# Attention backward: one dS unit in eight transposed by TensorE, with three smaller moves of loads and stores

## The chip, the cores and the metric

One core of one Trainium2 chip. The metric is the device time of one execution in microseconds. The kernel before took 2856.8 us (median of three runs, 2853.1 to 2865.4).

Names of engines in the profile: PE is TensorE's matmuls, PEld its weight loads, DVE is VectorE, ACT is ScalarE, POOL is GpSimd, SPq is the queue of DMA commands that SyncE issues. L1286 is a line of the kernel that ran; the changed kernel has other line numbers than the kernel before, so each fence says whose lines it shows. "..." in a fence or in code marks what is left out. The "built program" is the list of instructions that a kernel is built into.

## The reference, cut to what matters

A transformer block with adaptive layer norm (S = 2048, D = 512, 32 heads of 16, F = 1792, bf16), forward and all gradients.

```python
def _A_ref(x, wqkv, wo):                      # attention
    ...
    scores = einsum('bhqd,bhkd->bhqk', q, k) * scale
    p = softmax(scores)
    return einsum('bhqk,bhkd->bhqd', p, v)... @ wo
def _B_ref(x, w1, b1, w2, b2):                # MLP with squared relu
    ...
x = x + ga * _A_ref(layernorm(x) * (1 + ca) + sa, wqkv, wo)
x = x + gb * _B_ref(layernorm(x) * (1 + cb) + sb, w1, b1, w2, b2)
# returned: x and the gradients to x, wqkv, wo, w1, b1, w2, b2, c, w_mod
```

The argument is about the backward of the attention. For each head, each chunk of 512 keys and each block of 128 queries it recomputes the scores and their exp, forms dP = dO V^T, then dS = P * dP, and uses dS twice: as it is for dK, and transposed for dQ. The transposed dS is the tile `dsT`.

## The kernel before

A "unit" is two heads by 128 queries by 512 keys; there are 1024 of them in the backward. Four units make a group (G = 4), and one DMA transpose turns the whole group. `stp` gives two score buffers of one PSUM bank each, `dpp` two dP buffers of two banks each; with one bank each for `acckv` and `accq` all eight banks are used.

```python
dtp = tile_pool(name="p5dt", bufs=4)                       # dsT
stp = tile_pool(name="p5st", bufs=2, space=PSUM)           # scores
dpp = tile_pool(name="p5dp", bufs=2, space=PSUM)           # dP
...
def turn(g, jp, kvT):                       # 16 times in all: dK, dV of two heads
    tp = dpp.tile([P, ST, P], BF16, name="dp")
    for st in range(ST):
        nc.tensor.transpose(tp[:, st, :], kvT[:, st * P:(st + 1) * P], self.ident[:])
    ...                                     # two copies out by ACT
def dS(dp, u):
    (T, g, jp, c, ib, kvT, pu, dsg, i) = u
    nc.vector.tensor_tensor(dsg[:, i], dp[:], pu[:], ALU.mult)
    pend.append((T, g, jp, c, ib, kvT, pu, dsg[:, i]))
    if i == G - 1:
        dsT = dtp.tile([P, 8 * G, P], BF16, name="dsT")
        nc.sync.dma_start_transpose(dsT[:], dsg[:].rearrange("p i a k -> p (i a k)"))
        for i in range(G):
            pendq.append((T, g, jp, c, ib - G + 1 + i, i, dsT))
...
for i in range(G):                          # the loop over the units of a group
    for a in range(2):
        stt = stp.tile([P, 512], F32, name="st")
        nc.tensor.matmul(stt[:], lhsT=T["QT"][rs, q], rhs=masked["KT"]...)     # scores
        if last:
            dP(dp, last, a)                                                    # dP of the unit before
        nc.scalar.activation(pu[:, a, :], stt[:], ACT.Exp, scale=self.scale)
    if last:
        dS(dp, last)
    last = (T, g, jp, c, ib, kvT, pu, dsg, i)
    if i % 2 == 1 and len(pend) >= 4:
        r = kv_two()                        # dV and dK of two units
        ...
    elif i % 2 == 0 and len(pendq) > 2 * G:
        for _ in range(4 if len(pendq) > 3 * G else 2):
            dq(pendq.pop(0), [0, 1])        # 8 matmuls each, on dsT
```

The softmax here doesn't subtract the row's maximum and nothing guards it: scores larger than these inputs give would overflow.

## Time and profile before

| | before |
|---|---|
| time, median | 2856.8 us |
| backward, first to last score matmul | 1454.8 us |
| waits for dsT (as the view of that tile adds them) | 337.7 us, 238 times |
| TensorE at half clock from the first score to the last dq, in whole windows of 3.41 us | 170.7 us |
| from the last score matmul to the end | 145.9 us |

The prediction shows the lines that this rests on. One more view is used, the busy time in one stretch inside the backward. Its columns are the stretch, its length, busy microseconds (and instructions) of each engine, TensorE's mean granted clock, the busy share of the DMA engines and what they moved in GB/s. For the kernel before:

```profile
core 0: us, PE busy (x) PEld busy (x) DVE busy (x) ACT busy (x) POOL busy (x), PEclk, DMA share, GB/s
1300.00:2700.00 1400.00, 1227.44 (x15997) 502.25 (x15997) 1209.69 (x1062) 1079.93 (x1999) 0.00 (x0) 0.94 1.14 203
```

To see: the clock of 0.94, and 203 GB/s with the DMA engines' share above one (transfers overlap).

### The profile page before, as it was taken

To read this page: it belongs to the slowest core of one execution; us is meant where nothing else is said; L and a number is where in the kernel's file an instruction comes from. 1 tells how busy PE (TensorE), PEld (TensorE's weight loads), DVE (VectorE), ACT (ScalarE), POOL (GpSimd) and SP (SyncE) were. 2 spreads that over 40 slices of the span, in tenths; PEclk is the share of its full clock that TensorE was granted. 3 is DMA by queue.
4 is the path that set the end of the run, shared out by engine and by line. 5 is a ranking of instruction groups with operands and counts; after the bars stand their busy time and mean duration, and the time that the engine had idled before them with its cause. 6 is when DMAs were issued, how large, how long until landed. Compare 5 with 4: busy or idle time off the path is not lost. (4 is left out here: it accounts for less than half of the span.)

```text
span 2853.7 us, 72244 instructions
## 1 busy us (share of the span) xinstructions
PE 2530.8 (89%) x29963; PEld 1218.3 (43%) x30186; DVE 1787.2 (63%) x2712; ACT 2214.1 (78%) x3376; POOL 360.7 (13%) x633
## 2 busy tenths in 40 slices
PE   5999799999999989978888898888988889889887
PEld 2555455555555545723333333333333333333343
DVE  4222423323322335648898888888988889889747
ACT  4999899999999974248787777787877778778623
POOL 2244202211311223420000000000000000000021
PEclk9999899999999999989899999999999999999999
DMA  4367733511531357989999999999999999999977
GB/s 149 88 147 161 172 70 107 123 45 40 137 83 43 100 151 175 194 192 201 211 195 203 203 196 209 199 201 210 196 208 203 199 209 198 204 204 205 214 194 187
DMA packets 1331345, 472.86 MB, mean 166 GB/s; under 512 B 1266470, under 2 KB 1293608, under 8 KB 1331016
## 3 DMA queue, kind: packets, MB, share of 16 engines
q1 hardware_dynamic: 1299816, 379.40, 72.5%
q0 software_dynamic: 29088, 86.21, 10.4%
q8 instruction: 236, 3.87, 0.5%
q10 hardware_dynamic: 2112, 2.62, 0.3%
q14 instruction: 93, 0.76, 0.1%
HBM read 83.30 MB, written 67.11 MB: 53 GB/s over the span
## 5 line engine op out<-in xcount | busy, mean ns | idle before, releaser
L1269 ACT ACTIVATE pu<-st 128x512 bf16<-128x512 f32 x2048 | 1108.3, 595 | 313.8 <-PE dp L1218 279.6
L1223 DVE TENSOR_TENSOR ds<-dp,pu 128x1024 bf16<-128x1024 f32 x1024 | 1213.1, 1220 | 198.2 <-PE dp L1218 161.9
L331 ACT ACTIVATE pu<-st 128x1024 bf16<-128x1024 f32 x1024 | 955.7, 1046 | 22.5 <-PE st L328 18.0
L328 PE MATMUL st<-QTm,KTq 128*128 128x512 bf16 x1940 | 586.5, 379 | 37.2 <-ACT pu L331 7.5
L293 PEld LDWEIGHTS <-pu 128*128 128x128 bf16 x8192 | 344.9, 96 | 245.8 <-issue 20.5
L1265 PE MATMUL st<-m,q 64*128 64x512 bf16 x1024 | 371.4, 404 | 21.4 <-ACT pu L1269 9.6
L1265 PE MATMUL st<-m,QTq 64*128 64x512 bf16 x1024 | 365.0, 396 | 16.0 <-ACT pu L1269 4.4
L1218 PE MATMUL dp<-m,q 64*128 64x512 bf16 x1024 | 373.5, 408 | 0.0
L1199 PEld LDWEIGHTS <-dsT 128*128 128x128 bf16 x8192 | 241.1, 97 | 307.1 <-DMA dsT<-ds 189.8
L1218 PE MATMUL dp<-m,dOTq 64*128 64x512 bf16 x1024 | 366.4, 401 | 0.0
L293 PE MATMUL accbank<-Vaug,pu 128*128 128x17 bf16 x8192 | 349.3, 171 | 18.3 <-DVE O L301 11.4
L328 PEld LDWEIGHTS <-KTq 128*128 128x128 bf16 x2048 | 194.9, 96 | 205.8 <-issue 140.7
L1199 PE MATMUL accq<-Kg,dsT 128*128 128x16 bf16 x4096 | 143.6, 171 | 83.1 <-DMA dsT<-ds 82.8
L1199 PE MATMUL accq<-q,dsT 128*128 128x16 bf16 x4096 | 144.5, 171 | 65.6 <-DMA dsT<-ds 65.1
L1434 POOL DMA_DIRECT2D wmod<-in_w_mod_dram x6 | 4.6, 772 | 1462.1 <-DVE kvT L1182 1455.9
L1179 PE MATMUL acckv<-ds,q 128*16 128x512 bf16 x1024 | 165.3, 405 | 0.0
L1179 PE MATMUL acckv<-pu,q 128*16 128x512 bf16 x1024 | 165.3, 405 | 0.0
L1179 PE MATMUL acckv<-ds,Qg 128*16 128x512 bf16 x1024 | 162.1, 398 | 0.7 <-DVE ds L1223 0.7
L1179 PE MATMUL acckv<-pu,dOg 128*16 128x512 bf16 x1024 | 162.1, 398 | 0.0
L1218 PEld LDWEIGHTS <-q 64*128 64x128 bf16 x1024 | 90.8, 94 | 112.0 <-issue 101.4
L1218 PEld LDWEIGHTS <-dOTq 64*128 64x128 bf16 x1024 | 89.8, 94 | 103.3 <-issue 94.1
L300 DVE RECIPROCAL rl<-accbank 128x4 f32<-128x4 f32 x128 | 23.0, 179 | 164.8 <-PE accbank L293 164.7
(309 smaller groups left out, 2345.3 us busy)
## 6 DMA issues: line engine op xcount, KB each, us to landing
KTq<-KTq_d POOLq DMA_DIRECT2D x24, 512.0 KB, 3.6
duT_d<-auT POOLq DMA_DIRECT2D x4, 1792.0 KB, 8.3
aT_d<-rT POOLq DMA_DIRECT2D x4, 1792.0 KB, 13.0
KTq_d<-KTq SPq DMA_DIRECT2D x32, 128.0 KB, 2.1
QTq_d<-ev_fm SPq DMA_DIRECT2D x32, 128.0 KB, 2.4
VTq_d<-vT POOLq DMA_DIRECT2D x4, 1024.0 KB, 6.6
O_d<-O POOLq DMA_DIRECT2D x4, 1024.0 KB, 5.4
m<-KTq_d SPq DMA_DIRECT2D x32, 128.0 KB, 3.7
```

The costliest lines, as they stand in the source:

```text
L293: nc.tensor.matmul(acc[:, a, sub, :], lhsT=pu[:, a, sub * P:(sub + 1) * P], rhs=Vaug[:, kb, h, :], start=(kb == 0 and a == 0 and sub == 0) ...
L300: nc.vector.reciprocal(self.rl[:, st0:st0 + 4, h], acc[:, a, :, DH])
L328: nc.tensor.matmul(stt[:, a, :], lhsT=KT[:, kb * P:(kb + 1) * P], rhs=QTm[2 * jp + a][:], start=True, stop=True)
L331: nc.scalar.activation(pu[:], stt[:], ACT.Exp, scale=self.scale)
L1179: nc.tensor.matmul(acckv[r:r + DH, :], lhsT=T[n][:, ib, col:col + DH], rhs=src[:, a, :], start=(ib == 0), stop=(ib == ST - 1))
L1199: nc.tensor.matmul(accq[:, ib, a, :], lhsT=dsT[:, (i * 2 + a) * 4 + sub, :], rhs=T["K"][:, 4 * c + sub, col:col + DH], start=(c == 0 and i ...
L1218: nc.tensor.matmul(dp[:, a, :], lhsT=T["dOT"][rd, ib * P:(ib + 1) * P], rhs=masked["VT"][2 * jp + a][rd, 512 * c:512 * (c + 1)], start=Tru ...
L1223: nc.vector.tensor_tensor(dsg[:, i], dp[:], pu[:], ALU.mult)
L1265: nc.tensor.matmul(stt[:], lhsT=T["QT"][rs, q], rhs=masked["KT"][2 * jp + a][rs, c0:c0 + 512], start=True, stop=True)
L1269: nc.scalar.activation(pu[:, a, :], stt[:], ACT.Exp, scale=self.scale)
L1434: nc.gpsimd.dma_start(wmod[:], wmod_v[:, :, j * D:(j + 1) * D])
```

## The change

The intent: take load off the queue of DMA transposes, which bounds the backward, by letting TensorE turn one unit in eight (the first unit of every second group). Three small parts come with it: the load and scaling of W2 in three parts in the forward, all four weight tiles for dx loaded at once in the transition, and in the tail an earlier start of the dx tiles and a store on another queue.

```diff
             def dS(dp, u):
-                    dsT = dtp.tile([P, 8 * G, P], BF16, name="dsT")
-                    nc.sync.dma_start_transpose(dsT[:], dsg[:].rearrange("p i a k -> p (i a k)"))
+                    i0 = len(grp)
+                    dsT = grp[0] if i0 else dtp.tile([P, 8 * G, P], BF16, name="dsT")
+                    nc.sync.dma_start_transpose(dsT[:, 8 * i0:, :], dsg[:, i0:].rearrange("p i a k -> p (i a k)"))
 ...
+            def turn_ds(dsg, grp):
+                dsT = dtp.tile([P, 8 * G, P], BF16, name="dsT")
+                tp = stp.tile([P, 8, P], BF16, name="st")
+                for b in range(8):
+                    nc.tensor.transpose(tp[:, b, :], dsg[:, 0, b // 4, b % 4 * P:(b % 4 + 1) * P], self.ident[:])
+                nc.scalar.copy(dsT[:, 0:4, :], tp[:, 0:4, :])
+                nc.vector.tensor_copy(dsT[:, 4:8, :], tp[:, 4:8, :])
+                grp.append(dsT)
 ...
+                                if i == G - 1 and ib0 // G % 2:
+                                    turn_ds(dsg, grp)
 ... W2, in gen_weights and gen_weights_2
-        nc.sync.dma_start(w2[:], io["B_w2"].rearrange("(ft p) j -> p ft j", p=P))
+        self.load_w2(0, 5)
 ...
-        for ft in range(FT):
-            nc.vector.tensor_tensor(w2[:, ft, :], w2[:, ft, :], self.mod_row(5), ALU.mult)
-            if ft % 2:
-                yield 0
+        cuts = [0, 5, 10, FT]
+        for (a, b) in zip(cuts, cuts[1:]):
+            if b < FT:
+                self.load_w2(b, min(b + 5, FT))
+            for ft in range(a, b):
+                nc.vector.tensor_tensor(w2[:, ft, :], w2[:, ft, :], self.mod_row(5), ALU.mult)
+            yield ("wait", 4)
 ... dx weights: w_kt from a pool of four buffers, all loads and scalings first, transposes later
 ... tail
-            for _ in range(8):
+            for _ in range(5):
                 run("b", gb)
 ...
-            nc.sync.dma_start(io["out_9"]..., o[:])
+            nc.gpsimd.dma_start(io["out_9"]..., o[:])
```

More of the change, by code (lines that the diff above doesn't have):

```diff
@@ L720, in last_chunk @@
         fill.until("half")
-        self.load_bwd()
-        for _ in self.load_wmt():
-            fill.take(13)
+        ws = self.load_wmt(self.open_pool("wkt", bufs=1))
+        self.T0, pieces = self.load_group(0)
+        pieces = self.pair_pieces(0, 0) + pieces
+        for n, (d, sr) in enumerate(pieces):
+            nc.sync.dma_start(d, sr)
+            fill.take(7)
+            if n % 3 == 2 and ws:
+                self.turn_wmt(*ws.pop(0))
+        for w in ws:
+            self.turn_wmt(*w)
         fill.drain()
-        for name in ("dw2", "dw1", "e0", "dwps", "tps", "mps"):
+        for name in ("wkt", "dw2", "dw1", "e0", "dwps", "tps", "mps"):
             self.close_pool(name)
@@ L857, in gen_weights, with load_w2 @@
             yield 0
+    def load_w2(self, a, b):
+        self.nc.sync.dma_start(self.w2[:, a:b, :], self.io["B_w2"].rearrange("(ft p) j -> p ft j", p=P)[:, a:b, :])
     def gen_weights_1(self):
@@ L1100, in open_bwd, with load_wmt @@
         self.qp = self.open_pool("p5q", bufs=1, side="right")
-    def load_bwd(self):
-        nc = self.nc
-        self.T0, pieces = self.load_group(0)
-        for (d, sr) in self.pair_pieces(0, 0) + pieces:
-            nc.sync.dma_start(d, sr)
-    def load_wmt(self):
+    def load_wmt(self, sb):
         nc, io = self.nc, self.io
@@ L1112, in load_wmt, with turn_wmt @@
         self.WmT = self.wp.tile([P, 3 * DT, D], BF16, name="WmT")
+        ws = []
         for kt in range(DT):
-            w = self.wp.tile([P, 3 * D], BF16, name="w_kt")
+            w = sb.tile([P, 3 * D], BF16, name="w_kt", bufs=DT)
             nc.sync.dma_start(w[:], io["A_wqkv"][kt * P:(kt + 1) * P, :])
             nc.scalar.activation(w[:], w[:], ACT.Copy, scale=self.opcaT[:, kt:kt + 1])
-            yield
-            nc.sync.dma_start_transpose(self.WmT[:, :, kt * P:(kt + 1) * P], w[:])
-            yield
+            ws.append((kt, w))
+        return ws
+    def turn_wmt(self, kt, w):
+        self.nc.sync.dma_start_transpose(self.WmT[:, :, kt * P:(kt + 1) * P], w[:])
     def load_group(self, g):
@@ L1215, in dP @@
             def dP(dp, u, a):
-                (T, g, jp, c, ib, kvT, pu, dsg, i) = u
+                (T, g, jp, c, ib, kvT, pu, dsg, i, grp) = u
                 rd = slice(64 - 64 * jp, 128 - 64 * jp)
@@ L1221, in dS @@
             def dS(dp, u):
-                (T, g, jp, c, ib, kvT, pu, dsg, i) = u
+                (T, g, jp, c, ib, kvT, pu, dsg, i, grp) = u
                 nc.vector.tensor_tensor(dsg[:, i], dp[:], pu[:], ALU.mult)
@@ L1251, in attn_bwd @@
                                 nc.sync.dma_start(*pieces.pop(0))
-                            dsg = self.dsp.tile([P, G, 2, 512], BF16, name="ds")
+                            dsg, grp = self.dsp.tile([P, G, 2, 512], BF16, name="ds"), []
                             for i in range(G):
@@ L1271, in attn_bwd @@
                                     dS(dp, last)
-                                last = (T, g, jp, c, ib, kvT, pu, dsg, i)
+                                last = (T, g, jp, c, ib, kvT, pu, dsg, i, grp)
                                 if i % 2 == 1 and len(pend) >= 4:
@@ L1456, in gen_p7 @@
                     nc.scalar.activation(o[:, kt, :], dm[:], ACT.Copy, scale=self.scT[:, kt:kt + 1])
-            nc.sync.dma_start(io["out_9"].rearrange("(kt p) n -> p kt n", p=P)[:, :, j * D:(j + 1) * D], o[:])
+            nc.gpsimd.dma_start(io["out_9"].rearrange("(kt p) n -> p kt n", p=P)[:, :, j * D:(j + 1) * D], o[:])
             for kt in range(DT):
```

## The prediction

> **What bounds the kernel now.** I read the slices of the page first. They split the 2853.7 us into a forward part (to about 1050, ACT full), a transition (to 1258), the attention backward (1258 to 2711) and a tail. The backward is half the time and everything in it looks busy, so I asked for the groups of instructions, then for all that touches the tile dsT, then for the queue of SP and the order of time.
>
> The page and the groups with their shapes kept apart:
>
> ```profile
> PEclk9999899999999999989899999999999999999999
> DMA  4367733511531357989999999999999999999977
> ...
> L1223 DVE TENSOR_TENSOR ds<-dp,pu 128x1024 bf16<-128x1024 f32 x1024 | 1213.1, 1220 | 198.2 <-PE dp L1218 161.9 <-ACT pu L1269 15.6 <-ACT dv_t L1192 1.9
> ...
> L1199 PEld LDWEIGHTS <-dsT 128*128 128x128 bf16 x8192 | 241.1, 97 | 307.1 <-DMA dsT<-ds 189.8 <-issue 117.2
> ```
>
> To see: DMA is at nine tenths or more through the whole backward, and what TensorE waits for is dsT, the transposed dS.
>
> What touches dsT, then the queue of SP in a stretch of the backward:
>
> ```profile
> L1227 SPq DMA_TRANSPOSE dsT<-ds x256: 4777/5246/6183, 1264.0 to 2711.3; - x128
> ...
>   DMA dsT<-ds: 337.7, 238
> ...
> DMA to landing us min/median/max: 6.6/7.7/11.5
> ```
>
> ```profile
> 1896.89 0.57 SPq L1251 DMA_DIRECT2D m<-KTq_d  x1
> 1897.55 5.31 SPq L1227 DMA_TRANSPOSE dsT<-ds  x1
> 1902.92 0.57 SPq L1251 DMA_DIRECT2D m<-KTq_d  x1
> 1903.58 4.92 SPq L1227 DMA_TRANSPOSE dsT<-ds  x1
> 1908.55 0.57 SPq L1251 DMA_DIRECT2D m<-VTq_d  x1
> ```
>
> To see: the queue has no hole. 256 transposes by 5.25 is 1344 us, 121 loads by 0.57 another 71; together 1415 of 1452 us. The queue of transposes is the bound of the backward, by a little.
>
> How small the margin is shows in the order of time. A pair of units (two heads, two blocks of 128 queries) starts at 1900.31 and the next at 1902.73:
>
> ```profile
> 1900.31 0.39 PE L1265 MATMUL st<-m,QTq 64*128 64x512 bf16 x1
> ...
> 1900.73 2.14 ACT L1269 ACTIVATE pu<-st 128x512 bf16<-128x512 f32 x4 [0.28 <-PE dp L1218]
> ...
> 1901.38 0.37 PE L1265 MATMUL st<-m,QTq 64*128 64x512 bf16 x1
> ...
> 1901.87 0.37 PE L1265 MATMUL st<-m,QTq 64*128 64x512 bf16 x1
> ...
> 1902.73 0.39 PE L1265 MATMUL st<-m,QTq 64*128 64x512 bf16 x1
> ```
>
> To see: scores at 0, two exps to 1.49, the last scores of the pair at 1.56 (they need the buffer that the second exp frees), dP and dV/dK, next pair at 2.42. This TensorE-ACT loop gives 512 x 2.42 = 1239 us without any dsT wait. VectorE does a dS every 1.13 us back to back (smallest spacing in the trace), 2.26 per pair, so it sits just under.
>
> I counted all pairs in the trace. The 1450 us of the backward are: 1241 clean loop; about 118 of TensorE standing for dsT; about 46 of half clock (157 us at half clock; a pair wholly in it takes 3.43, so each us costs 0.29); 32 for the 16 turns of kvT (3.76 + 3.08 against 4.84: 2.0 each); some 13 for the rest. 34 of the 40 half-clock stretches begin within 2.2 us after a hole of over 1.3 us in TensorE, nearly always a dsT wait: the clock is lost to the same waits.
>
> **What the Trainium skill says.** "TensorE: Matmul & The Clock Gate", Part 1 (What's actually happening): the clock is either half or full, decided by activity over windows of 3413 ns. The trace agrees: stretches of 3.4 or 6.8 us at 0.5. The same page, Part 4 (PE-mode transpose): a transpose ends in PSUM and must be copied out, and does not count as TensorE activity the same way. The copies are in the trace; that it costs clock is not: 15 of the 16 kvT turns (16 transposes each, with holes of 0.3 to 0.5 about them) are followed by no half clock. "DMA: Bandwidth & Descriptors", Issuing engines are not separate DMA queues: all queues share 16 engines, so moving the stores of the last output to the GpSimd queue gives only order, no bandwidth. And "PSUM — Partial Sum Buffer", Specifications: a bank is 2 KiB per partition; the turned 8 x 128 bf16 fill one, exactly one of the two score buffers.
>
> **The change part by part.**
>
> Backward. In every second group of four units, the first unit is transposed by TensorE, so 128 DMA transposes shrink from 32 blocks to 24: 128 x 5.25/4 = 168 us off the queue. Per eight units it then needs 5.25 + 3.94 + 0.6 of loads = 9.8 us against a clean loop of 9.7; with the turn the loop is longer than the queue, and dsT arrives (0.6 lag + 7.7) before its use two groups later (about 10). The 118 + 46 us of waits and half clock should go, except perhaps 15.
>
> Added are 128 turns: 8 transposes, an ACT copy and a VectorE copy of 128x512. Their rows before are those of the kvT turn and of the forward's turns:
>
> ```profile
> 1349.60 1.05 PE L1188 MATMUL dp<-ident,kvT 128*128 128x128 bf16 x16 [0.28 <-DVE ds L1223]
> ...
> 1350.69 0.58 ACT L1192 COPY dk_t<-dp 128x512 bf16<-128x512 bf16 x1 [1.10 <-PE dp L1188]
> ```
>
> ```profile
> L577 DVE COPY fT<-tp x4: 405/426/426, 1042.5 to 1060.2; 128x512 bf16<-128x512 bf16 x4
> ```
>
> To see: half of the 16 transposes is some 0.54, the copies 0.58 and 0.43. They follow dV/dK at the end of a pair, so the next pair starts 0.54 late. The copies hold one of the two score buffers: ACT copies until 0.69 after that start; VectorE, which stands at its dS until then, until about 0.69 too. The second scores of the next unit thus come at 0.75 instead of 0.23, their exp ends at 1.77, the last scores of the pair come at 1.84 instead of 1.56: another 0.28. (The same working gives 3.08 for the pair after a kvT turn, as measured.) So 0.82 per turn. In half of the turns VectorE is some 0.4 late from a kvT copy (0.74 against 0.16 of slack per pair): 0.36 more. Mean 1.0, in all 128 us, of which I take 122.
>
> New backward: 1241 + 122 + 32 + 13 + 15 = 1423, that is 27 less.
>
> W2 in three parts (around 300 to 370 us). Before, 12 scalings stand ahead of the copy-out of O, and TensorE stands 5.5 us for it:
>
> ```profile
> PE accbank L293 <- DVE O L301: 8.7, 3, 5.5
> ```
>
> In the changed order on VectorE the first scaling stands between the reciprocal and the copy-out of the block before, and there it must wait for its load: 640 of 1792 KB, estimated landing 5 us after issue (10.6 before), then the small b2 load some 3 us later. The copy-out comes some 7 us late, one block earlier than now. The second and third part are loaded after the transpose of Wo and their nine scalings stand ahead of another copy-out: some 5 us more and 2 of half clock. I expect the wait to move and not to go: +5. By the delay, 16 matmuls more are left over after the forward loop: +2.
>
> dx weights in four buffers (1214 to 1258). TensorE stood 9.2 us for a_blk, ACT for each w_kt in turn, and the first exp of the backward waited 4.2 for the last of them. All four loads now go first; the traffic is the same (3.8 MB and eight transposes), only the chain at the end goes: -5.
>
> Tail. The dx tiles start after five blocks instead of eight, and the stores leave the queue that feeds dqT. TensorE is busy 113 us of the last 130, eight or nine of idle at the end can't go; so -5, and -3 because the last dsT (11.5 us after issue now) has 24 blocks.
>
> Sum: -27 + 7 - 5 - 8 = -33, and 2856.8 - 33 = 2824. I go to 2818, because the turns may cost 0.82 throughout.
>
> **The rivals.** (1) The queue was the whole bound and the turns hide in the loop's slack: then -164 + 15 in the backward and about 2700. Against it: the loop has no slack, the score buffer is its critical resource. (2) VectorE becomes the bound: 8 x 1.13 + 0.43 + 0.46 (kvT, dq) = 9.94 per eight units, under 10.7; if its dS is really 1.19 apart it is 10.4, still under. It would give about 2810 to 2830. (3) The turns trip the half clock: 3.4 x 0.29 = 1 us per turn, +128, about 2940. Against it: the kvT turns. (4) The W2 wait does go: 10 us better, about 2808.
>
> **Range and chances.** The size of a turn moves most: 0.25 us either way is 32 us. W2, transition and tail together are good for 15. I give 2778 to 2850. Faster by over 2% (under 2800) needs turns of about 0.8 and one of the small parts to do well: 0.27. Within 2%: 0.70. Slower: 0.03.
>
> **What would show it.** Right: dsT waits under 30 us where they were 338; mean clock of the backward near 0.99 instead of 0.94; pairs with a turn of about 2.96, and 2.70 after it; the queue of SP with holes; a wait for the copy-out of O one block earlier. Wrong: dsT waits over 100 us, pairs longer than 3.3 around a turn, VectorE without holes, or half clock after turns.

## The result, and the profile after

The changed kernel took 2849.5 us (median of four, 2847.6 to 2852.9), against 2857.4 us for the kernel before in the same rounds: ratio 0.9971, interval [0.9946, 0.9995]. Run a second time on another chip in five rounds it gave 0.9981 [0.996, 1.0002]. So the kernel is 5 to 8 us faster, or in the second measurement not told apart from the kernel before; predicted were 39 (2856.8 to 2818). The interval is a 95% interval.

What the change aimed at did happen. The slices of the page of the changed kernel:

```profile
PEclk9999999999999999989999999999999999999999
DMA  4367632520531266989999999999999999999986
```

The same stretch of its backward as above:

```profile
1300.00:2700.00 1400.00, 1271.06 (x17074) 564.47 (x17074) 1259.76 (x1192) 1162.48 (x2135) 0.00 (x0) 1.00 0.99 181
```

The clock is 1.00 and the DMA moves 181 GB/s instead of 203. The view of the tile dsT of the changed kernel (durations are least, median and greatest, in ns):

```profile
L1238 SPq DMA_TRANSPOSE dsT<-ds x256: 3566/4766/5948, 1263.1 to 2705.2; - x128
...
  ACT dsT L1248: 30.4, 81
  DMA dsT<-ds: 9.9, 11
...
DMA to landing us min/median/max: 5.4/6.8/9.4
```

Waits for dsT fell from 337.7 to 9.9 us and the half clock of the backward from 170.7 to 13.7 us (10.2 of it at the very start of the backward, 3.4 after the last score). But the backward, from first to last score matmul, went only from 1454.8 to 1449.3. The gain was spent in the same place.

Where it went shows in the length of pairs of units, counted from the first score matmul after a dV/dK to the next such. A plain pair has no transpose in it or just before it; a kvT turn is the `turn` of dK and dV shown above. I went through all 508 pairs of each trace:

| pair | before | after | after, all such pairs above 2.42 us each |
|---|---|---|---|
| plain | 478 pairs, 2.42 us but up to 6.6 where it waits | 239 pairs, 2.42 us | 4 us |
| ends in a turn of dS | none | 112 pairs, 2.98 us | 66 us |
| starts after a turn of dS | none | 127 pairs, **3.16 us** | 96 us |
| kvT turn | 15 pairs 3.76, then 15 pairs 3.08 | 15 pairs 3.76, then 15 pairs 3.64 (kvT and dS turn) | 38 us |
| sum of all pairs | 1440.9 us | 1435.7 us | |

The prediction had 2.96 for the pair with a turn and 2.70 for the one after it. The first is right, the second is not. The order of time around one turn of the changed kernel (start, length, engine, line; what ended its idle time in brackets):

```profile
1911.79 0.62 PE L1247 MATMUL st<-ident,ds 128*128 128x128 bf16 x8
...
1912.35 0.39 PE L1286 MATMUL st<-m,QTq 64*128 64x512 bf16 x1
...
1912.45 0.58 ACT L1248 COPY dsT<-st 128x512 bf16<-128x512 bf16 x1 [0.48 <-PE st L1247]
...
1913.07 0.42 DVE L1249 COPY dsT<-st 128x512 bf16<-128x512 bf16 x1 [0.29 <-ACT dsT L1248]
1913.59 0.37 PE L1286 MATMUL st<-m,QTq 64*128 64x512 bf16 x1 [0.85 <-ACT pu L1290]
```

To see: VectorE's copy does not run beside ACT's copy, it waits for it. And the second score matmul of the pair, the last line, comes 1.24 us after the first. Its bracket names an exp, and rightly. I looked up in the built program which PSUM bank each of these uses and what it waits for:

```
PE   first scores    -> bank 1, waits for an exp of the unit before
ACT  copy, blocks 0-3 <- bank 0 (the turned tile), waits for PE
DVE  copy, blocks 4-7 <- bank 0, waits for ACT's copy
ACT  exp of the first scores <- bank 1
PE   second scores   -> bank 1 again, waits for that exp
```

This is so at all 127 turns that have scores after them. There are two score buffers. The turned tile has one of them until both copies are done; the other is taken by the first scores, whose exp stands behind the copy in ACT's queue. Over all turns the medians after the start of the pair are: ACT copy 0.10 to 0.69, VectorE copy 0.72 to 1.15, second scores 1.24 (0.05 after that exp, 0.09 after VectorE's copy). Whichever buffer they take, they cannot come much before 1.2. The prediction had both copies done at 0.69 and the scores at 0.75, in the buffer of the turn.

The W2 wait moved and stayed, as predicted. In the view of waits of the changed kernel from 298 to 400 us (total, times, longest):

```profile
PE accbank L293 <- DVE O L301: 9.3, 3, 4.6
```

### The profile page after: what moved, and what is told of

Same layout as the page of the kernel before. It is cut to its first block, busy times and chain, and to the rows that moved or that the text cites. A ratio compares the mean times of both kernels' runs of the same rounds, so it can differ in the third digit from the quotient of the medians.

```text
span 2845.7 us, 74675 instructions
## 1 busy us (share of the span) xinstructions
PE 2590.2 (91%) x31210; PEld 1280.3 (45%) x31210; DVE 1830.7 (64%) x2840; ACT 2293.5 (81%) x3504; POOL 365.0 (13%) x639
## 5 line engine op out<-in xcount | busy, mean ns | idle before, releaser
L1290 ACT ACTIVATE pu<-st 128x512 bf16<-128x512 f32 x2048 | 1125.6, 596 | 210.0 <-PE dp L1228 115.7
L328 PE MATMUL st<-QTm,KTq 128*128 128x512 bf16 x2048 | 611.6, 380 | 30.5 <-ACT pu L331 7.7
L1286 PE MATMUL st<-m,q 64*128 64x512 bf16 x1024 | 362.7, 382 | 68.2 <-ACT pu L1290 61.1
L1228 PE MATMUL dp<-m,q 64*128 64x512 bf16 x1024 | 364.3, 387 | 0.0
L1189 PE MATMUL acckv<-ds,Qg 128*16 128x512 bf16 x1024 | 154.0, 381 | 0.6 <-DVE ds L1233 0.6
L1189 PE MATMUL acckv<-ds,q 128*16 128x512 bf16 x1024 | 154.5, 382 | 0.0
L1189 PE MATMUL acckv<-pu,q 128*16 128x512 bf16 x1024 | 154.5, 382 | 0.0
L1189 PE MATMUL acckv<-pu,dOg 128*16 128x512 bf16 x1024 | 154.0, 381 | 0.0
```

The source lines that it names most:

```text
L328: nc.tensor.matmul(stt[:, a, :], lhsT=KT[:, kb * P:(kb + 1) * P], rhs=QTm[2 * jp + a][:], start=True, stop=True)
L1189: nc.tensor.matmul(acckv[r:r + DH, :], lhsT=T[n][:, ib, col:col + DH], rhs=src[:, a, :], start=(ib == 0), stop=(ib == ST - 1))
L1228: nc.tensor.matmul(dp[:, a, :], lhsT=T["dOT"][rd, ib * P:(ib + 1) * P], rhs=masked["VT"][2 * jp + a][rd, 512 * c:512 * (c + 1)], start=Tru ...
```

## The experiments

Seventeen kernels ran, the changed one twice. "Backward" is the sum of the 508 pairs; the rightmost column is the median of that pair. All give correct results except the two marked as wrong.

| kernel | ratio to before | backward | waits for dsT | pair after a turn |
|---|---|---|---|---|
| before | 1 | 1440.9 | 337.7 | |
| the changed kernel | 0.9971 | 1435.7 | 9.9 | 3.16 |
| turn in a dP buffer, two banks | 0.9796 | 1383.3 | 41.1 | 2.59 |
| the same, one bank | 0.9815 | 1387.1 | 53.9 | 2.59 |
| two PSUM tiles | 0.9802 | 1379.1 | 37.6 | 2.58 |
| half a unit turned | 0.9833 | 1398.8 | 101.4 | 2.66 |
| no turn, 24 blocks by DMA (wrong) | 0.9593 | 1328.9 | 145.8 | |
| no turn, 16 blocks by DMA (wrong) | 0.9375 | 1266.3 | 1.0 | |
| turns alone | 0.9996 | 1438.3 | 17.0 | 3.16 |
| small parts alone | 1.0016 | 1441.0 | 335.9 | |
| dP buffer, VectorE copy alone | 0.9797 | 1384.8 | 49.1 | 2.58 |
| dP buffer, DMA in two pieces | 0.9784 | 1374.0 | 12.7 | 2.68 |
| before, DMA in two pieces | 1.0168 | 1484.2 | 259.1 | |
| dP buffer, one unit in 16 | 0.9822 | 1389.3 | 172.9 | 2.60 |
| VectorE copy, two pieces, no small parts | 0.9774 | 1377.9 | 17.2 | 2.68 |
| two tiles, two pieces, no small parts | 0.9777 | 1374.8 | 16.9 | 2.68 |
| the changed kernel, tail undone | 0.9986 | 1438.5 | 12.2 | 3.16 |
| the changed kernel again | 0.9981 | 1437.5 | 12.1 | 3.16 |

### The turned tile in a dP buffer, its halves in two banks

My first theory came from the Trainium skill, "PSUM — Partial Sum Buffer", section "PSUM bank collisions raise a hardware error": the compiler back end adds a dependency between any two instructions on different engines that touch the same bank and quadrant of partitions, reads included. The halves of the turned tile lie in one bank.

```diff
-                tp = stp.tile([P, 8, P], BF16, name="st")
+                tp = dpp.tile([P, 16, P], BF16, name="dp")
-                    nc.tensor.transpose(tp[:, b, :], ...)
+                    nc.tensor.transpose(tp[:, b // 4 * 8 + b % 4, :], ...)
-                nc.vector.tensor_copy(dsT[:, 4:8, :], tp[:, 4:8, :])
+                nc.vector.tensor_copy(dsT[:, 4:8, :], tp[:, 8:12, :])
```

> The changed kernel with the turned tile in a dP buffer instead of a score buffer, its two halves in two PSUM banks. Theory 'bank': in the changed kernel the turn costs 1.30 us and not 0.82 because both halves of the turned tile lie in one bank that is also a score buffer, so the VectorE copy waits for the ACT copy (0.3 to 0.4 us) and the second scores of the next unit wait for both. Then here the wait of the VectorE copy for ACT is gone from the tile view of dsT, the pair after a turn falls from 3.16 us to 2.70 to 2.80, the pair with a turn stays at 2.98, and the time is 45 to 58 us under the changed kernel, about 2798. Rival 'engine time': the pair is late because ACT spends 0.58 us and VectorE 0.42 us more in it; then the pair after a turn stays at 3.05 to 3.2 and the time is within 12 us of the changed kernel.

Measured: 2793.8 us, ratio 0.9796 [0.9773, 0.9818], the pair after a turn 2.59 us. The gain is there, but not for the reason given. The order of time around a turn:

```profile
1914.31 0.62 PE L1247 MATMUL dp<-ident,ds 128*128 128x128 bf16 x8
...
1914.87 0.39 PE L1286 MATMUL st<-m,QTq 64*128 64x512 bf16 x1
...
1914.97 0.59 ACT L1248 COPY dsT<-dp 128x512 bf16<-128x512 bf16 x1 [0.27 <-PE dp L1247]
...
1915.30 0.39 PE L1286 MATMUL st<-m,QTq 64*128 64x512 bf16 x1
...
1915.59 0.42 DVE L1249 COPY dsT<-dp 128x512 bf16<-128x512 bf16 x1 [0.34 <-ACT dsT L1248]
```

To see: with the halves in two banks VectorE's copy still waits for ACT's (128 of 128 times, 41.5 us in all). But the second scores start 0.43 after the first, before either copy is done: no score buffer is held, so each of the two scores has its own. So the wait is not about the bank, and it costs nothing by itself (the pair is 2.58 in the run below in which the copies overlap).

### The same with one bank

The edit is the first line of the one above only.

> As the run before it, with the turned tile in a dP buffer, but all eight blocks in one bank. It splits the theory in two. If the price is the hold of the score buffer, this kernel does as well as the one with two banks (pair after a turn 2.70 to 2.80, about 2798), though its VectorE copy still waits about 0.3 us for ACT. If the serial copies cost time by themselves, the pair after a turn is 3.0 to 3.1 and the time about 2830. In both cases the wait of the VectorE copy for the ACT copy must be there; if it is not, it is not a matter of the bank.

Measured: 2799.2 us, 0.9815 [0.9793, 0.9837]; the pair after a turn 2.59, the wait of VectorE's copy for ACT's 40.0 us. Same as with two banks within the intervals. What costs is that the turn takes a score buffer; the run with two tiles, below, adds that it is the time for which it is held. The rival that ACT's and VectorE's own time makes the pair late falls: they do the same copies here.

### Half a unit turned

Four blocks, one ACT copy, still in a score buffer; the DMA takes 28 of 32.

```diff
-                for b in range(8):
+                for b in range(4):
...
-                nc.scalar.copy(dsT[:, 0:4, :], tp[:, 0:4, :])
-                nc.vector.tensor_copy(dsT[:, 4:8, :], tp[:, 4:8, :])
+                nc.scalar.copy(dsT[:, 0:4, :], tp[:])
```

> The changed kernel with only the first four of the eight blocks of the unit turned by TensorE, copied by ACT alone, still in a score buffer; the DMA takes 28 of 32 blocks. There is one copy, so nothing to be put in series. Theory: 0.28 us of transposes in the pair with a turn (2.70), a hold of the score buffer until about 0.7 after the start of the next pair, which makes that pair 2.70; 128 x 0.56 = 72 us for all turns instead of 166, and a DMA queue of 1331 us that stays below the loop. With some 20 us for new waits for dsT: 65 to 90 us under the changed kernel, about 2770. Rival: a turn has a fixed price (a hole in TensorE and a late exp), the pair after it stays above 2.95 and the gain is under 40 us; or the DMA queue bounds again and waits for dsT come back to over 60 us.

Measured: 2804.4 us, 0.9833 [0.9809, 0.9857]. The pair after a turn is 2.66 as expected; the pair with a turn is 2.86 in the median, not 2.70. In the built program the second scores go to the buffer of the turn, wait for the one copy (done at 0.67) and come at 0.72. The time is a miss, by 34 us: the waits for dsT came back, which the rival had in part.

```profile
  DMA dsT<-ds: 101.4, 97
```

### No turn, and 24 blocks by DMA (wrong)

The changed kernel without `turn_ds`; dq of that unit reads another unit's blocks, so the result is wrong.

> Wrong on purpose (dq of one unit in eight is summed from another unit's blocks): the changed kernel with its 24-block DMA transposes but with no turn on TensorE and no copies. It shows the price of the turns in place and the clean loop. If the turns cost 1.30 us each as counted by pairs (128 x 1.30 = 166), the time is 2849 - 166 = 2683, pairs are 2.42 throughout but for the kvT turns, and waits for dsT stay under 30 us (queue 1247 us of about 1286). If the turns hide a wait that comes back without them (VectorE at 1.13 us per dS, or the DMA queue), it is above 2720.

Measured: 2736.0 us, 0.9593 [0.9572, 0.9615]. The expected 2683 is missed by 53 us, the alternative (above 2720) came, and it is the most useful result: taking away turns that cost about 169 us (by the clean run below) gained 113 (107 in the backward), because waits for dsT reappeared, though the commands of the queue (1181 us of transposes and 68 of loads) take less than the backward:

```profile
  DMA dsT<-ds: 145.8, 131
```

The waits are thus not only those of a full queue. They grow as the loop comes near to it.

### No turn, and 16 blocks by DMA (wrong)

```diff
-                    nc.sync.dma_start_transpose(dsT[:, 8 * i0:, :], dsg[:, i0:]...)
+                    nc.sync.dma_start_transpose(dsT[:, 16:, :], dsg[:, 2:]...)
```

> Wrong on purpose (half of the blocks of dS are not transposed; dq takes others): no turns, and every DMA transpose has 16 blocks instead of 32, which takes the queue far below the loop. It gives the clean loop of the backward, which the prediction put at 1241 + 32 + 13 = 1286 us from first to last pair. If so, waits for dsT are under 10 us and the time is about 2849 - 150 = 2700; the run without turns (1329 us, 146 us of waits for dsT) was then 43 us above it because its queue, 1242 us of work, is too near to the loop. If the loop is slowed by something else (VectorE, the clock), it stays above 1305 us and 2715.

Measured: 2672.0 us, 0.9375 [0.9359, 0.9391]; backward 1266.3 us, or 1279.9 from the first to the last score where 1286 was expected. The time is 28 us under the expected 2700: the expectation's gain of 150 us is the changed kernel's sum of pairs (1436) less 1286, which is from the first to the last score, another measure.

```profile
1300.00:2700.00 1400.00, 1314.46 (x16688) 572.19 (x16696) 1288.78 (x1318) 1125.38 (x2091) 38.76 (x58) 0.99 0.68 130
```

To see: the DMA's share is 0.68, the clock 0.99 (the end of the stretch already lies in the tail). This is the clean loop. From it every other backward can be read as a sum: before 1266.3 + 174.6 of DMA waits and half clock; the changed kernel 1266.3 + 169.4 for 128 turns, 1.32 us each, and hardly a wait. The two numbers are almost the same, and that is the whole result.

### Two PSUM tiles

This tells a score buffer held for long from one held at all. In the built program VectorE's copy now waits for PE alone, and the second scores go to the buffer of the turn, which ACT's copy frees.

```diff
-                tp = stp.tile([P, 8, P], BF16, name="st")
+                tp, tq = stp.tile([P, 4, P], BF16, name="st"), dpp.tile([P, 4, P], BF16, name="dp")
...
-                nc.vector.tensor_copy(dsT[:, 4:8, :], tp[:, 4:8, :])
+                nc.vector.tensor_copy(dsT[:, 4:8, :], tq[:])
```

> The changed kernel with the turned blocks in two PSUM tiles: blocks 0 to 3 in a score buffer, copied by ACT, and blocks 4 to 7 in a dP buffer, copied by VectorE. In the built program the VectorE copy no longer waits for ACT, which it did still do in the run with two banks of one tile. Theory: the price of the pair after a turn (3.16) is the hold of the score buffer up to the end of the second, serial copy (1.24 after the start of the pair); here the hold ends with the ACT copy at about 0.7, so that pair is 2.65 to 2.75, between the 2.59 of the dP buffer alone and 3.16, the wait of the copy for ACT is under 5 us, and the time is 2797 to 2810. Rival: any hold of a score buffer by a turn costs the same, however short; then the pair stays above 3.0 and the time above 2830.

Measured: 2793.8 us, 0.9802 [0.9785, 0.9819], the pair after a turn 2.58.

```profile
1912.92 0.40 PE L1247 MATMUL st<-ident,ds 128*128 128x128 bf16 x4
...
1913.16 0.39 PE L1247 MATMUL dp<-ident,ds 128*128 128x128 bf16 x4
...
1913.36 0.59 ACT L1248 COPY dsT<-st 128x512 bf16<-128x512 bf16 x1
...
1913.48 0.39 PE L1286 MATMUL st<-m,QTq 64*128 64x512 bf16 x1
...
1913.71 0.41 DVE L1249 COPY dsT<-dp 128x512 bf16<-128x512 bf16 x1
...
1913.99 0.37 PE L1286 MATMUL st<-m,QTq 64*128 64x512 bf16 x1
```

To see: the two copies overlap. ACT's starts with the first four blocks, before the pair begins, and frees the score buffer 0.47 after it; the second scores come at 0.51 in that buffer. A score buffer is held here too, but shortly. VectorE's copy, no longer set behind ACT's, runs from 0.29 to 0.71 (medians). Had the copies of the changed kernel overlapped like this, the turned tile would have been free at about the 0.69 of the prediction.

### The turns alone, and the small parts alone

The kernel before with `turn_ds` only, and the changed kernel with the condition of the turn set to false.

> The kernel before with only the turns of dS added; W2, the dx weights and the tail as before. If the parts add up as in the stages of the traces: backward -5, last dsT with 24 blocks -4 in the tail, so 6 to 10 us under before (ratio 0.9965 to 0.998). If the three small parts carry the gain, it is within 3 us of before.

> The changed kernel without the turns: 32 blocks by DMA in each group, and the other three parts (W2 in three loads, four dx weight buffers, dx tiles after five blocks with the stores on another queue). The prediction gave these +7, -5 and -8 in all -6. From the stages of the trace after: W2 +1, transition +1, tail +2 or so without the earlier last dsT; so it should be within 4 us of before (ratio 0.9985 to 1.0015). If the prediction's own sizes hold, it is 6 us under (0.998).

Measured: turns alone 2850.2 us, 0.9996 [0.9981, 1.0011], a miss: 6 to 10 us under were expected, and 2 came (in the medians), within the band of the rival; small parts alone 2855.6 us, 1.0016 [0.9997, 1.0034]. The rival does not hold either, since the small parts alone carry no gain. Neither is told apart from before, and together they do not make the 0.9971 of the first measurement of the whole; the second measurement (0.9981, interval up to 1.0002) fits better. The waits for dsT with the turns alone are 17.0 us, so they do their work without the small parts.

### The dP buffer with VectorE's copy alone

```diff
-                nc.scalar.copy(dsT[:, 0:4, :], tp[:, 0:4, :])
-                nc.vector.tensor_copy(dsT[:, 4:8, :], tp[:, 4:8, :])
+                nc.vector.tensor_copy(dsT[:, 0:8, :], tp[:, 0:8, :])
```

> The changed kernel with the eight turned blocks in one dP tile and copied by VectorE alone, in one 128x1024 copy (estimate 0.83 us from two halves of 0.42). ACT, which paces the loop, gives nothing. Theory (the price of a turn is what it takes from TensorE and from the score buffers and ACT, and VectorE has slack): the pair with a turn stays at 2.98 and the pair after it falls from 2.59 in the dP run to about 2.42 to 2.50; the loop saves 127 x 0.1 to 0.16 = 13 to 20 us, of which waits for dsT give back up to half: 2780 to 2792. Rival: VectorE becomes the bound (8 x 1.13 + 0.83 + 0.23 of kvT = 10.1 of some 10.3 us per eight units), dP waits for its buffer, the pair after a turn stays at or above 2.6 and the time is at or above 2795.

Measured: 2794.9 us, 0.9797 [0.9762, 0.9832], the pair after a turn 2.58. My theory (2.42 to 2.50, at most 2792 us) missed; the result lies at the edge of the rival (2.6, 2795 us). No gain over the two copies, so the rest of 0.16 us above 2.42 is not ACT's. The order of time:

```profile
1916.53 0.39 PE L1285 MATMUL st<-m,QTq 64*128 64x512 bf16 x1
...
1916.82 0.68 DVE L1248 COPY dsT<-dp 128x1024 bf16<-128x1024 bf16 x1
...
1916.97 0.39 PE L1285 MATMUL st<-m,QTq 64*128 64x512 bf16 x1
```

To see: the second scores come at 0.44 here, and the dP matmul just ahead of them starts only at 1916.96: it needs the other dP buffer, which VectorE's dS leaves when this copy begins. That this is what sets the 2.58 I infer from the order; no run tests it alone. The copy of 1024 columns takes 0.68 us, less than two of 512 (0.84).

### The dP buffer, with the DMA transposes in two pieces

16 and 16 blocks, or 8 and 16 in a group with a turn, each issued as soon as its dS is there.

```diff
-                if i == G - 1:
-                    i0 = len(grp) ...
-                    nc.sync.dma_start_transpose(dsT[:, 8 * i0:, :], dsg[:, i0:]...)
+                i0 = ib // G % 2
+                if i == 1:
+                    grp.append(dtp.tile([P, 8 * G, P], BF16, name="dsT"))
+                if i % 2:
+                    dsT, b0 = grp[0], max(i - 1, i0)
+                    nc.sync.dma_start_transpose(dsT[:, 8 * b0:8 * i + 8, :], dsg[:, b0:i + 1]...)
```

> The dP version (two banks of one tile) with each DMA transpose issued in two pieces, the first two units of a group as soon as their dS is there: 16 + 16 blocks, and 8 + 16 in a group with a turn. Waits for dsT were 41 us with whole groups. If the waits come from the uneven queue (one long piece per group), they fall under 15 us and the time by 5 to 20 us, to 2775 to 2790. If the queue is bound by blocks (0.16 us each), the earlier issue can only smooth; no change within 5 us. If each issue has a fixed cost above its blocks, the queue gets longer and the waits grow to over 80 us, about 2820.

Measured: 2789.3 us, 0.9784 [0.976, 0.9808]; backward 1374.0. The tile view:

```profile
  DMA dsT<-ds: 12.7, 13
...
DMA to landing us min/median/max: 3.1/4.7/6.9
```

The waits fell from 41.1 to 12.7 us, as the first case expected, since a piece lands after 4.7 us and not 6.9. The time is only 4.5 us less in the median and the intervals overlap: the median pair after a turn became longer in exchange, 2.68 against 2.59.

### The kernel before, with the DMA transposes in two pieces

> The kernel before with only this: each DMA transpose of 32 blocks is issued as two of 16. In the run with 16 blocks per group one took 1.91 us on the queue, against 5.25 for 32; if that rate held for all, the queue would shrink from 1344 to about 980 us and no turn would be needed: waits for dsT under 20 us and about 2690. That run had holes in its queue, so I rather expect that the engines behind it are the limit: two pieces take 5.0 to 5.4 us together, the waits stay within 80 us of the 338 before, and the time is within 1.5% of before (2815 to 2870).

Measured: 2901.3 us, 1.0168 [1.0141, 1.0195]; slower, outside what I expected, though two pieces take 5.27 us together, as expected. The waits for dsT fell to 259.1 us, but in the list of who waited for that tile's instructions (total, times) there is a new one:

```profile
  DVE ds L1223: 126.5, 82
```

The stretch of the backward, in the columns of above:

```profile
1300.00:2700.00 1400.00, 1241.28 (x15587) 494.63 (x15584) 1167.50 (x1035) 1065.84 (x1951) 0.00 (x0) 0.94 1.14 197
```

The DMA moves no more than before, 197 GB/s, and VectorE waits for buffers of dS, which the transposes still read. So the rate of 1.91 us for 16 blocks was that of a queue with holes. I read the two figures, 203 and 197 GB/s at a share of 1.14, as the limit of the DMA engines in this kernel; averaged over its backward, no run here moved more. Cutting the transposes alone does not replace TensorE's turns. Why the buffers come free later than with one piece stays open.

### One unit in sixteen

```diff
-                                if i == G - 1 and ib0 // G % 2:
+                                if i == G - 1 and ib0 // G % 4 == 3:
```

> The dP version with one unit in sixteen turned instead of one in eight. Turns cost half: 64 x 0.73 = 47 us instead of 93. The queue gets 84 us of blocks back: 1344 - 84 + 71 = 1331 us, of a loop of 1266 + 47 = 1313: it is the bound again. Theory (turn costs and queue waits trade against each other, so that fewer turns give back as waits what they save): backward 1375 to 1400, waits for dsT 110 to 190 us, time 2785 to 2810. If waits for dsT only came from the full queue of before, and go with any relief, it is 2750 to 2770.

Measured: 2803.6 us, 0.9822 [0.9794, 0.9851], backward 1389.3, waits for dsT 172.9 us: as expected in all three. Half the turns cost about 47 us less and the waits gave it back.

### Both cheap turns without the small parts

The kernel before with the pieces of above and the turn either in a dP buffer with one VectorE copy, or in two tiles.

> The kernel before (W2, dx weights and tail as before) with the turns in a dP tile copied by VectorE alone (0.68 us for 128x1024) and each DMA transpose in two pieces. From the runs so far: backward 1374 with the same pieces and the two copies; here ACT gives nothing and VectorE 0.68 instead of 0.85, so 1365 to 1378. If the three small parts of the change gave nothing (the run with them alone was 1.0016 of before), this is as good as the best so far or better: ratio 0.974 to 0.979. If they were worth the 6 us of the prediction, it is behind it: 0.980 to 0.982.

> The same base with the turned blocks split over a score buffer (ACT copy) and a dP buffer (VectorE copy), and the DMA transposes in two pieces. Pair after a turn 2.58 as in the run with two tiles, waits for dsT under 15 us as in the run with pieces: backward 1370 to 1380, ratio 0.974 to 0.979, within 0.3% of the run with the VectorE copy alone.

Measured: 2792.3 us, 0.9774 [0.9749, 0.9798], and 2792.8 us, 0.9777 [0.9754, 0.9799]; the times as expected, but the pair after a turn is 2.68 (2.58 expected for two tiles) and the waits for dsT 17 us (under 15 expected). These and the dP version with two pieces are the best kernels, about 2% under both the kernel before and the changed one (2848.8 us on the same chip). They can't be told from one another, and so the small parts are worth nothing that these rounds could show.

### The tail undone, and the changed kernel again

> The changed kernel with the tail of before (dx tiles after eight blocks, stores of the last output on the queue of SP). The prediction gave this part -5 us. If so, this kernel is 5 us over the changed one. From the trace of the run with the small parts alone, where the time from the last dq to the end was 135.3 us against 129.8 before, I expect the opposite: 1 to 5 us under the changed kernel, in the span from the last dq to the end 128 to 131 us instead of 132.5.

> The changed kernel itself once more, for a closer ratio to before and beside the kernel with the tail undone on the same chip: 0.996 to 0.9995. Its parts alone gave 0.9996 (turns) and 1.0016 (the rest), so if they add, it is near 1.000; if the first measurement holds, 0.997.

Measured: 2850.6 us, 0.9986 [0.9964, 1.0008], and 2848.8 us, 0.9981 [0.996, 1.0002]. The expectation of 1 to 5 us under the changed kernel is not met, and neither is the prediction's 5 us over it. From the last score to the end it is 145.2 us with the old tail and 146.0 with the new one. Inconclusive: below what can be measured.

## Why the prediction was right or wrong

The time was wrong: 39 us of gain forecast, 8 measured, and 6 in the repeat. That 2849.5 us lies just within the range given, and "within 2%" came, is owed to the width of the range and not to the working: the mean price of a turn, on which the forecast rests, was wrong. By its own steps:

**What bounds the kernel: right.** The clean loop was put at 1241 for 512 pairs and 32 for the kvT turns; the run with 16 blocks has 1266.3 for 508 pairs with 15 kvT turns (1231 + 30 by the prediction's figures). The 118 + 46 us of DMA waits and half clock measure 174.6.

**The waits and the half clock go: right**, 337.7 to 9.9 us and 170.7 to 13.7 us of half clock. Of the 15 us held back for waits, hardly any came: the plain pairs of the changed kernel are together 4 us longer than 2.42 us each, those of the run with 16 blocks 5. The queue of SP is busy for 1220 of 1446 us. No half clock after turns: right; no half-clock window begins within 7 us of the start of any of the 128.

**The price of a turn: this is the step that failed.** "The copies hold one of the two score buffers: ACT copies until 0.69 after that start; VectorE ... until about 0.69 too. The second scores of the next unit thus come at 0.75". That a score buffer is what counts was right. The overlap of the two copies was wrong, and with it the size of the term. The two copies read one PSUM tile and the built program sets them in series, so the tile is held until 1.15; and the second scores are given the other buffer, that of the first scores, whose exp comes after ACT's copy. They come at 1.24, and the second part of the turn's price is 0.74 us instead of 0.28. The first part was 0.56, against 0.54. With the measured terms the sum closes: first to last score 1279.9 in the clean run, plus the turns' 66 + 96 + 8 (the 15 turns after a kvT turn) = 170, is 1450; measured 1449.3. The prediction had 122 there. Its loop without turns was 6 us too long (1241 + 32 + 13 against 1279.9) and its 15 us of waits hardly came, so by luck 21 of the 48 us of error were hidden. Nor was there the 0.36 us more that half of the turns were to cost because VectorE comes late from a kvT copy: all 127 pairs after a turn lie between 3.16 and 3.33. The runs with the turn in a dP buffer and in two tiles show that this is the term: there the second part is 0.16, less than had been predicted. That the built program takes the other buffer because the series makes the turn's buffer late is my reading; no run shows the choice alone (a turn in a score buffer with one copy of all eight blocks was not tried), and either buffer was free only at 1.15 to 1.19. Both the series and the buffer could be read in the built program without a run; I read the diff and not that.

**The forecast inside the range of turns.** "The turns may cost 0.82 throughout" moved the forecast from 2824 to 2818, the wrong way.

**W2: right in kind.** The wait for the copy-out of O moved by a block (8.7 us in 3 waits before, 9.3 in 3 after). The size was +5; at the start of block 20 of the 64 of the forward the changed kernel is 0.7 us behind (377.0 against 376.3). The leftover matmuls: the first matmul of the last chunk's MLP starts at 1064.4 instead of 1060.7, but the weight gradients after it begin at the same time (1121.9 and 1121.7).

**Transition: -5 not found.** From the start of the second weight gradient to the first full pair it takes 78.6 us, before 78.0. All four loads come first, but TensorE still stands 9.9 us in three waits for the activations of the weight gradient (11.6 in three before), and the first exp comes only 1 us earlier.

**Tail: -8 not found.** From the last score to the end 145.9 us before, 143.8 after, 146.0 in the repeat. The last dsT did come earlier (dq ends 11.4 us after the last score instead of 16.0), and the rest took it back (132.4 instead of 129.9). But that rest is 131.5 us with the turns alone, 133.8 with the tail undone and 134.7 in the repeat, so 2 us in single traces tell nothing, and which store or load would have taken it is not shown.

**The rivals.** None of them came. For the first (turns that hide, about 2700) there is now a measure: with turns that cost nothing the kernel is at 2736, as the run without turns shows. VectorE did not become the bound (busy 1260 of 1400 us in the stretch shown) and no half clock followed the turns.

## What to carry to other kernels

When a transfer that bounds a loop is moved to an engine inside the loop, price it by how long it holds the buffer that the loop turns on, and look in the built program which buffer the next step is given and whether the copies that free it really run side by side; two engines that read one PSUM tile may be put in series even from two banks. Where two limits lie close together, the longer one alone does not give the time: here (1249 us of commands on the queue, 1266 of clean loop) taking away 169 us of turns gave 107 in the backward, and the rest came back as waits for the queue. A unit whose halves go to two tiles, or to the buffer with the slack, made the same change worth 2%.

## What the Trainium skill lacked or had wrong

- "PSUM — Partial Sum Buffer", section "PSUM bank collisions raise a hardware error", speaks of dependencies by bank and quadrant. In this kernel's built program they follow the tile: with the halves of one tile in two banks VectorE's copy waited for ACT's 128 times of 128 (41.5 us), with two tiles never. Nothing was seen to contradict the rule on banks itself.
- "DMA: Bandwidth & Descriptors", section "Latency and other measured facts", gives 261 GB/s for a DMA transpose on one kernel. Transposes between SBUF tiles with some loads beside them moved no more than 203 GB/s, averaged over the backward, in any run here (5.25 us on the queue for 32 blocks of 128x128 bf16), and cutting them in two raised nothing (197 GB/s, 1.7% slower). The layouts may differ; what sets the limit is not shown.
- "TensorE: Matmul & The Clock Gate", section "HAM oscillation — how this bites in real kernels", warns of idle gaps of over 3.4 us. Here shorter ones went with the half clock: 34 of 40 half-clock stretches before began within 2.2 us after a hole of over 1.3 us, and the longest hole was 3.36 us. The 128 turns, with a hole of 0.85 us in the one shown, were followed by none (13.7 us at half clock in all, at the start and the end of the backward).
